# When the weight sums of an attention and feed-forward kernel may begin, and where in the third tile they stand

## The chip, the cores and the metric

One core of a Trainium2 chip runs the kernel. The metric is device time in microseconds (us). Engines: PE multiplies matrices, DVE (VectorE) and ACT (ScalarE) work element by element, POOL (GpSimd) and SP (SyncE) here mostly issue DMA transfers. Each engine takes its instructions strictly in the order of its own queue.

## The reference

```python
# attention in chunks of 64 positions, 8 x 8 heads, 576 positions, 64 wide
scores = scale * np.matmul(q_c, k_c.transpose(0, 1, 2, 4, 3))
scores = scores - np.max(scores, axis=-1, keepdims=True)
attn = np.exp(scores)
attn = attn / (np.sum(attn, axis=-1, keepdims=True) + 1e-09)
out = np.matmul(attn, v_c)
# its output becomes x, 4608 tokens x 512; w_in is 512 x 2048, w_out 2048 x 512
h = x @ w_in
g = np.where(h >= 1, h, np.where(h <= -1, 0.0, (h + 1) ** 2 / 4))
return (g @ w_out).astype(np.float32)
```

Everything is float32.

## The kernel before, in words

**Tiles.** The 4608 tokens are nine tiles of 512. For each the attention of its heads is computed, then h and g in 16 slices of 128 columns, j = 0 to 15, then the output. Each float32 factor is split into a high and a low part, and three products (high with high, high with low, low with high) replace one. `ffn_in` (line 610) issues the 12 products of a slice into a bank `ps_h`; ACT and DVE make g from it in a buffer `r` (lines 617, 620, 621); `ffn_split` makes its high part `gh` on ACT (line 629) and the low part `gl` on DVE (line 631); `ffn_out` (line 646) adds 12 products into four banks `ps_o`, two slices later. There are two buffers each of `ps_h`, `r`, `gh` and `gl`. I write I0, I1, ... and O0, O1, ... for input and output products, numbered 16 t + j: I16 and O16 are the first of tile 1, O32 the first of tile 2. V and S are the value and score products of the attention for coming tiles, put in between as bursts; each burst is followed by a row maximum (`mx`), eight exponentials on ACT, sums (`sm`) and transposes on DVE, and small moves of the results (`aT`, line 565, on POOL or SP).

**Two ways of multiplying.** Tiles 0, 1 and 2 are computed as said. Tiles 3 to 8 go in pairs by a scheme with seven products in place of eight, which needs sums and differences of blocks of the weights. These are made during tiles 1 and 2, each from two slices of a weight: `combine_weights(p)` for w_in, p = 0 to 7, called w0 to w7 below, and `combine_out(p)` for w_out, called o0 to o5 (two more follow in tile 3). Each consists of two first adds on DVE, four half-width adds, two roundings on ACT, two subtractions on DVE (lines 728 and 732), and then stores to DRAM that POOL issues: seven for w (line 838, four from the staging tiles and three of raw weight parts), four for o (line 986). Besides, `keep_factor` (line 961) stores 24 raw pieces of w_out to DRAM. Tile 3 and later load all of it back through rings.

**Staging tiles.** The sums are made in four tiles of 128 x 512, `tmp0` to `tmp3`, in two pairs (shown as `tmp_135` and `tmp_136`). The same four receive the output of tiles 0, 1 and 2 from `ps_o` (`store`, DVE line 660, ACT line 662), from where SP stores it (line 667); a bank `ps_o` is free for the next tile once its copy is made. Banks 0 and 3 are copied into pair 0, banks 1 and 2 into pair 1; banks 0 and 2 by ACT, 1 and 3 by DVE. In tile 2 every second sum uses another pair of stages, `alt` (`new_wi_0`, `new_wi_1`), instead: those whose step is in `AGAIN`.

**What sets the order.** All work is first recorded with `plan.add(engine, cost, emit, reads, writes, ...)`. `Plan.emit` then runs a simple simulation: an entry becomes ready when the entries that wrote its keys are done, and each engine takes, of its ready entries, the one with the smallest turn, which is its place in the record less `ahead`. Sums of w_out and raw stores have `ahead=LATER`, that is 60 places behind. The order in which the plan takes entries is the order of the hardware queues. On the chip an instruction waits for the data that it reads and the buffers that it writes. The step of the record is (t - 1) * 16 + j; the main loop calls the sums at the steps in `SUMS_AT` and `WEIGHTS`:

```python
ffn_split(t, j)
if step in WEIGHTS:
    combine_weights(WEIGHTS.index(step), step in AGAIN)
if step in SUMS_AT:
    combine_out(SUMS_AT.index(step), step in AGAIN)
if t == 1:
    for name in ("P4",) if j % 2 else ("P1", "P2"):
        keep_factor(name, j // 2)
```

In the record a raw store thus stands in tile 1, but it reads only a slice of w_out that was prepared in tile 0, so the plan may take it as soon as POOL has nothing else ready.

Of the kernel before, what the change touches and what calls it, by code (L numbers as in the profile page):

```python
# [9 lines left out]
F32 = mybir.dt.float32  # L10
# [123 lines left out]
def kernel(  # L134
# [15 lines left out]
    nc = tc.nc  # L150
# [85 lines left out]
    weight = {}  # L236
# [27 lines left out]
    plan = Plan()  # L264
# [3 lines left out]
    def now(ap):  # L268
        return ap() if callable(ap) else ap
# [355 lines left out]
    def ffn_split(t, j, source=None, ahead=0):  # L625
        rkey, r = source or r_bufs[j % 2]
        ghkey, gh = gh_bufs[j % 2]
        glkey, gl = gl_bufs[j % 2]
        plan.add("act", 0.52, lambda: nc.scalar.copy(out=gh, in_=now(r)), (rkey,), (ghkey,),  # L629
                 ahead=ahead)  # L630
        plan.add("dve", 0.6, lambda: nc.vector.tensor_tensor(  # L631
            out=gl, in0=now(r), in1=gh.bitcast(F32), op=ALU.subtract
        ), (rkey, ghkey), (glkey,), port=True, ahead=ahead)
# [85 lines left out]
    def cols(n):  # L719
        return slice(n * QC, (n + 1) * QC)  # L720
# [5 lines left out]
    def act_copy(cost, out, src, reads, writes, ahead=0):  # L726
        plan.add(
            "act", cost, lambda: nc.scalar.copy(out=out(), in_=src()), reads, writes, ahead=ahead  # L728
        )
# [59 lines left out]
    def stage_of(again):  # L789
        if again:  # L790
            some = [(f"alt{n}_{i}", part_of(f"alt{n}", i)) for n in range(2) for i in range(2)]
            return *some, [lambda n=n: held[f"alt{n}"] for n in range(2)]
        return *((key, fixed(ap)) for key, ap in tmp_bufs), [fixed(pair) for pair in tmp_pairs]

    def combine_weights(p, again=False):
        js = (2 * p, 2 * p + 1)
        keys = [[f"wi{j}_{n}" for n in range(2)] for j in js]
        (k1, w1), (k12, s12), (k2, w2), (k34, s34), pairs = stage_of(again)

        def kc(ap, n):  # L800
            return lambda: ap().rearrange("p (i two f) -> p two i f", i=2, two=2)[:, n]

        def two(ap, n):
            return lambda: ap()[:, cols(n)].rearrange("p (i f) -> p i f", i=2)

        for j, ks, key, w in zip(js, keys, (k1, k2), (w1, w2)):
            dve(0.6, ALU.add, w, lambda j=j: weight["wi", j][:, 0, :].bitcast(F32),
                lambda j=j: weight["wi", j][:, 1, :].bitcast(F32), ks, (key,))
        a11, a12, a21, a22 = (kc(w, n) for w in (w1, w2) for n in range(2))
        dve(0.34, ALU.add, two(s12, 0), a21, a22, (k2,), (k12,))  # L810
        dve(0.34, ALU.subtract, two(s12, 1), two(s12, 0), a11, (k1,), (k12,))
        dve(0.34, ALU.subtract, two(s34, 0), a11, a21, (k1, k2), (k34,))
        dve(0.34, ALU.subtract, two(s34, 1), a12, two(s12, 1), (k1, k12), (k34,))
        for hkey, hi, key, ap in ((k1, w1, k12, s12), (k2, w2, k34, s34)):
            act_copy(0.52, rounded(hi), ap, (key,), (hkey,))
            dve(0.6, ALU.subtract, rounded(ap), ap, hi, (hkey,), (key, f"split_{p}"))
        st = [(k1, k12), (k2, k34)]

        def of_block(n, h):
            return lambda: weight["wi", js[n]].rearrange(  # L820
                "p x (i two f) -> p two x i f", i=2, two=2
            )[:, h]

        def of_stage(n, h):
            return lambda: pairs[n]()[:, :, cols(h)].rearrange("p x (i f) -> p x i f", i=2)

        for r, src, reads in (
            (2, of_stage(0, 1), st[0]), (3, of_stage(0, 0), st[0]),
            (5, of_stage(1, 0), st[1]), (4, of_stage(1, 1), st[1]),
            (0, of_block(0, 0), (*keys[0], f"split_{p}")), (1, of_block(0, 1), (*keys[0], f"split_{p}")),  # L830
            (6, of_block(1, 1), (*keys[1], f"split_{p}")),
        ):
            d, n = divmod(7 * p + r, 2)

            def send(d=d, n=n, src=src):
                dst = combos[d][:, n, :].rearrange("p (x i f) -> p x i f", x=2, i=2)
                ap = src()
                nc.gpsimd.dma_start(out=dst.bitcast(F32), in_=ap.bitcast(F32))

            plan.add("pool", 0.7, send, reads, (f"dram{d}_{n}",), lag=1.7, moving=0.8)  # L840
# [112 lines left out]
        for name in OUT_ORDER for p in range(NQ)  # L953
    }

    def keep_factor(name, p):
        n, half = RAW[name]
        j = 2 * p + n

        def send():  # L960
            nc.gpsimd.dma_start(  # L961
                out=sums[name, p].bitcast(F32), in_=weight["wo", j][:, :, cols(half)].bitcast(F32)
            )

        plan.add("pool", 0.7, send, (f"wo{j}_0", f"wo{j}_1"), (f"sums_{name}_{p}",), lag=3.0,
                 moving=0.8, ahead=LATER)

    def combine_out(p, again=False, behind=()):
# [343 lines left out]

    SPREAD = {1: (None, 8), 4: (8, 9), 7: (9, 10), 10: (10, 11), 13: (11, 12), 15: (None, 13)}
    SPREAD.update({NF + 2 * n: (12 + n, 14 + n) for n in range(8)})
    SUMS_AT = (0, 6, 12, 18, 20, 23)
    WEIGHTS = (2, 4, 8, 10, 14, 21, 26, 28)
    AGAIN = sorted(step for step in (*SUMS_AT, *WEIGHTS) if step > 17)[::2]

    def burst(n, m):
# [15 lines left out]
    for t in range(ALONE + 1):  # L1335
        for j in range(NF):
            step = (t - 1) * NF + j
            if t == 0:
                for what, g in SECOND.get(j, ()):
                    what(*divmod(NP + g, NP))  # L1340
            elif step in SPREAD:
                n, m = SPREAD[step]
                if n is None and m == 2 * NP:
                    attn_turn(*AT[m])
                burst(n, m)
                if m is not None and m + 1 <= 3 * NP + 1:
                    attn_turn(*AT[m + 1])
            ffn_in(t, j)
            prepare_next()
            m = t * NF + j - LAG  # L1350
            if m >= 0:
                ffn_out(*divmod(m, NF))
            ffn_split(t, j)
            if step in WEIGHTS:
                combine_weights(WEIGHTS.index(step), step in AGAIN)
            if step in SUMS_AT:
                combine_out(SUMS_AT.index(step), step in AGAIN)
            if t == 1:
                for name in ("P4",) if j % 2 else ("P1", "P2"):
                    keep_factor(name, j // 2)  # L1360
            if t == ALONE and j < len(HANDED):
                hand_lot("wi", j, F32 if j < 2 else F32R, *HANDED[j])
                if j == 2:
                    hand_lot("wo", 0, F32R, "ring0")
        if t:
            take_raws((first_raw, next_raw)[t - 1], t % 2)
# [17 lines left out]
    for t in range(ALONE + 1, NTILE, 2):  # L1384
        if t > ALONE + 1:
            move_blocks()
        for n, (p, name) in enumerate(alternating(0, NQ)):
            between(n)
            if t == ALONE + 1 and name == "P1":
                if p in (1, 4):  # L1390
                    combine_out(len(SUMS_AT) + p // 4, True, (blocks["eA", p - 1][0],))
                place_blocks(p)
# [69 lines left out]
```

## Time and profile before

| what | us |
|---|---|
| three runs | 819.76, 821.46, 821.82; median 821.46 |
| the profiled execution | 822.29 |
| its span in the trace | 820.5 |
| busy: PE, DVE, ACT, POOL | 808.1, 659.1, 537.6, 343.6 |
| first input product of tile 1 / of tile 2 | 126.87 / 222.17 |
| last output product of tile 2 ends | 326.24 |

The stretches are read as shares: PE busy for the whole of a slice means that nothing is lost there. A bracket at the end of a timeline row, [1.62 <-DMA ...], is the idle time of that engine ahead of the row, and what ended it. A DMA row at POOL or SP is the issue; when the data has landed is told by the DMA table, as a median per kind.

### The profile page before, as it was taken

To read this page: it belongs to the slowest core of one execution; us is meant where nothing else is said; L and a number is where in the kernel's file an instruction comes from. 1 tells how busy PE (TensorE), PEld (TensorE's weight loads), DVE (VectorE), ACT (ScalarE), POOL (GpSimd) and SP (SyncE) were. 2 spreads that over 40 slices of the span, in tenths; PEclk is the share of its full clock that TensorE was granted. 3 is DMA by queue.
4 is the path that set the end of the run, shared out by engine and by line. 5 is a ranking of instruction groups with operands and counts; after the bars stand their busy time and mean duration, and the time that the engine had idled before them with its cause. 6 is when DMAs were issued, how large, how long until landed. Compare 5 with 4: busy or idle time off the path is not lost.

```text
span 820.5 us, 18541 instructions
## 1 busy us (share of the span) xinstructions
PE 808.1 (98%) x6464; PEld 694.1 (85%) x6464; DVE 659.1 (80%) x1143; ACT 537.6 (66%) x1295; POOL 343.6 (42%) x606
## 2 busy tenths in 40 slices
PE   8999999999999999999999999999999999999998
PEld 7777778888888788878899998878999988888887
DVE  4999998778889986888899885778995845589963
ACT  5789876455676765778985446778844456686450
POOL 2133343345446463556454333554433333333330
PEclk9999999999999999999999999999999999999999
DMA  9999955765798796999999678987666876666673
GB/s 216 265 309 289 301 134 156 204 196 173 195 259 236 197 278 150 282 272 283 272 240 271 184 236 241 249 229 220 191 200 186 228 219 197 194 192 186 208 208 109
DMA packets 245356, 181.61 MB, mean 221 GB/s; under 512 B 192656, under 2 KB 210576, under 8 KB 245264
## 3 DMA queue, kind: packets, MB, share of 16 engines
q0 software_dynamic: 40640, 122.72, 48.0%
q1 hardware_dynamic: 202512, 57.18, 30.7%
q8 instruction: 52, 0.85, 0.4%
q10 hardware_dynamic: 2112, 0.52, 0.3%
q14 instruction: 40, 0.33, 0.2%
HBM read 133.17 MB, written 38.80 MB: 210 GB/s over the span
## 4 chain that ended last, share of the span: by engine, by line
PE 75%; DMA 9%; DVE 5%; SPq 5%; issue 2%; ACT 1%; POOL 1%; DVEq 0%; POOLq 0%; ACTq 0%
PE ps_o L1119 19%; PE ps_h L610 12%; PE ps_o L646 11%; PE ps_o L903 10%; PE ps_h L903 10%; PE ps_h L1119 8%; DMA q_sb<-in_q_dram 3%; PE ps_a L1119 3%; DMA words<-in_moe_w_in_dram 2%; SPq L382 2%; PE ps_a L487 2%; DMA k_sb<-in_k_dram 1%; PE ps_a L465 1%; DMA v_sb<-in_v_dram 1%; SPq L398 1%
## 5 line engine op out<-in xcount | busy, mean ns | idle before, releaser
L728 ACT CAST new_wi<-new_wi 128x512 fp32r<-128x512 f32 x156 | 94.5, 625 | 63.6 <-PE ps_o L1119 32.2
L732 DVE TENSOR_TENSOR new_wi<-new_wi,new_wi 128x512 fp32r<-128x512 f32 (+2 forms) x194 | 124.8, 673 | 13.2 <-ACT new_wi L728 12.9
L610 PE MATMUL ps_h<-xh,parts 128*128 128x512 f32 x384 | 130.0, 398 | 3.2 <-DVE parts L350 1.7
L646 PE MATMUL ps_o<-parts,gh 128*128 128x512 f32 x384 | 118.6, 390 | 0.0
L610 PEld LDWEIGHTS ps_h<-xh,parts 128*128 128x128 f32 x384 | 71.9, 188 | 20.1 <-DVE parts L350 2.6
L646 PEld LDWEIGHTS ps_o<-parts,gh 128*128 128x128 f32 x384 | 72.0, 188 | 14.9
L646 PE MATMUL ps_o<-parts,gl 128*128 128x512 f32 x192 | 74.8, 390 | 0.3 <-DVE gl L631 0.3
L565 POOL DMA_DIRECT2D aT<-e x96 | 48.2, 511 | 46.3 <-issue 13.6
L934 DVE SCALAR_TENSOR_TENSOR new_wi<-h,new_wi 128x512 f32<-128x512 f32 x62 | 41.8, 685 | 30.4 <-ACT new_wi L933 30.3
L532 ACT ACTIVATE e<-ps_a,mx 128x64 f32<-128x64 f32 x168 | 50.6, 328 | 11.6 <-DVE mx L526 8.2
L933 ACT ACTIVATE new_wi<-new_wi 128x512 f32<-128x512 f32 x84 | 51.6, 638 | 1.0
L610 PE MATMUL ps_h<-x_parts,parts 128*128 128x512 f32 x128 | 50.1, 392 | 0.0
L930 ACT ACTIVATE new_wi<-h 128x512 f32<-128x512 f32 x62 | 38.9, 641 | 13.0 <-DVE h L924 12.8
L629 ACT CAST gh<-r 128x512 fp32r<-128x512 f32 x48 | 29.9, 624 | 26.6 <-DVE r L621 18.9
L646 PEld LDWEIGHTS ps_o<-parts,gl 128*128 128x128 f32 x192 | 36.1, 188 | 8.3 <-DVE gl L631 0.8
L961 POOL DMA_DIRECT2D sums_P<-parts x24 | 17.8, 789 | 57.5 <-DVE parts L350 57.5
L732 DVE TENSOR_TENSOR new_wi<-new_wi 128x512 f32<-128x512 f32 (+2 forms) x64 | 40.2, 631 | 0.4
L631 DVE TENSOR_TENSOR gl<-r,gh 128x512 fp32r<-128x512 f32 x48 | 32.7, 684 | 7.6 <-ACT gh L629 7.0
L621 DVE SCALAR_TENSOR_TENSOR r<-ps_h,r 128x512 f32<-128x512 f32 x48 | 32.7, 683 | 7.2 <-ACT r L620 7.0
L532 ACT ACTIVATION_READ_ACCUMULATOR e<-ps_a,mx 128x1 f32 x168 | 37.2, 221 | 0.0
L1119 PE MATMUL ps_o<-new_wo,new_wi 128*128 128x256 f32 (+1 forms) x244 | 35.0, 293 | 0.0
L1119 PE MATMUL ps_o<-ring_r,new_wi 128*128 128x256 f32 (+1 forms) x244 | 34.6, 293 | 0.0
(260 smaller groups left out, 2158.8 us busy)
## 6 DMA issues: line engine op xcount, KB each, us to landing
ring_r<-combos POOLq DMA_DIRECT2D x36, 256.0 KB, 3.8
new_wo<-sums_P POOLq DMA_DIRECT2D x36, 256.0 KB, 3.3
new_wi<-combos POOLq DMA_DIRECT2D x34, 256.0 KB, 4.6
new_wi<-sums_P POOLq DMA_DIRECT2D x34, 256.0 KB, 3.2
ring_gh<-combos POOLq DMA_DIRECT2D x33, 256.0 KB, 4.0
ring_gl<-combos POOLq DMA_DIRECT2D x33, 256.0 KB, 3.9
ring_gh<-sums_P POOLq DMA_DIRECT2D x33, 256.0 KB, 3.3
ring_gl<-sums_P POOLq DMA_DIRECT2D x33, 256.0 KB, 3.5
```

Source lines behind the costliest of these rows:

```text
L532: nc.scalar.activation(out=e3[:, n, :], in_=sc[:, n // 4, n % 4, :], func=AF.Exp, bias=mx[:, n, :], scale=SCALE, accum_out=sm[:, n, :],)
L565: queues[queue].dma_start(out=aT[b:b + Q, to], in_=x[a:a + Q, of])
L610: nc.tensor.matmul(out=ps, lhsT=weight["wi", j][:, half, kc * P:(kc + 1) * P], rhs=x, start=(kc == 0 and i == 0), stop=(kc == KC - 1 and i ...
L621: plan.add("dve", 0.6, lambda: nc.vector.scalar_tensor_tensor(out=r, in0=ps, scalar=1.0, in1=r, op0=ALU.max, op1=ALU.min), (pkey,), (rkey,))
L646: nc.tensor.matmul(out=acc, lhsT=x[:, cols], rhs=weight["wo", j][:, half, :], start=(j == 0 and i == 0), stop=(j == NF - 1 and i == 2),)
L728: "act", cost, lambda: nc.scalar.copy(out=out(), in_=src()), reads, writes, ahead=ahead
L732: plan.add("dve", cost, lambda: nc.vector.tensor_tensor(out=out(), in0=one(), in1=two(), op=op), reads, writes, port=True, ahead=ahead)
L903: nc.tensor.matmul(out=ps, lhsT=w()[:, at:at + P], rhs=y(), start=name in FRESH and i == 0 and k == 0, stop=i == 1 and k == 2, skip_group_ ...
L930: plan.add("act", 0.52, lambda: nc.scalar.activation(out=now(r), in_=h(), func=AF.Relu, bias=0.5, scale=0.5), (hkey,), (rkey,), ahead=50)
L933: plan.add("act", 0.52, lambda: nc.scalar.square(out=now(r), in_=now(r)), (), (rkey,), ahead=50)
L934: plan.add("dve", 0.6, lambda: nc.vector.scalar_tensor_tensor(out=now(r), in0=h(), scalar=1.0, in1=now(r), op0=ALU.max, op1=ALU.min), (hke ...
L1119: nc.tensor.matmul(out=into, lhsT=x()[:, block], rhs=factor, start=first and k == 0, stop=p == NQ - 1 and k == len(steps) - 1, skip_group_ ...
```

## The change

`ffn_split`'s ACT copy now also writes a key `split_t_j`. The first adds of `combine_weights` and of `combine_out`, and the raw stores of `keep_factor`, read the key of the step at which they are recorded. In the plan, and by the wait that follows from it on the chip, they can't begin before the `gh` copy of that step. Two tables change: the sums o4 and o5 go from steps 20 and 23 to 23 and 28, w5, w6 and w7 from 21, 26 and 28 to 20, 25 and 30. In tile 2, steps 16 to 31, the sums then stand at 18, 20, 23, 25, 28 and 30. `AGAIN` follows from the tables: before {18, 21, 26} used the `alt` stages, after it is {18, 23, 28}. No instruction is added or removed.

```diff
@@ ffn_split
-        plan.add("act", 0.52, lambda: nc.scalar.copy(out=gh, in_=now(r)), (rkey,), (ghkey,),
-                 ahead=ahead)
+        plan.add("act", 0.52, lambda: nc.scalar.copy(out=gh, in_=now(r)), (rkey,),
+                 (ghkey, f"split_{t}_{j}"), ahead=ahead)
@@ combine_weights
-    def combine_weights(p, again=False):
+    def combine_weights(p, again=False, behind=()):
...
-                lambda j=j: weight["wi", j][:, 1, :].bitcast(F32), ks, (key,))
+                lambda j=j: weight["wi", j][:, 1, :].bitcast(F32), (*ks, *behind), (key,))
@@ keep_factor
-    def keep_factor(name, p):
+    def keep_factor(name, p, behind):
...
-        plan.add("pool", 0.7, send, (f"wo{j}_0", f"wo{j}_1"), (f"sums_{name}_{p}",), lag=3.0,
+        plan.add("pool", 0.7, send, (f"wo{j}_0", f"wo{j}_1", behind), (f"sums_{name}_{p}",), lag=3.0,
                  moving=0.8, ahead=LATER)
@@ the main loop
-    SUMS_AT = (0, 6, 12, 18, 20, 23)
-    WEIGHTS = (2, 4, 8, 10, 14, 21, 26, 28)
+    SUMS_AT = (0, 6, 12, 18, 23, 28)
+    WEIGHTS = (2, 4, 8, 10, 14, 20, 25, 30)
...
-                combine_weights(WEIGHTS.index(step), step in AGAIN)
+                combine_weights(WEIGHTS.index(step), step in AGAIN, (f"split_{t}_{j}",))
             if step in SUMS_AT:
-                combine_out(SUMS_AT.index(step), step in AGAIN)
+                combine_out(SUMS_AT.index(step), step in AGAIN, (f"split_{t}_{j}",))
             if t == 1:
                 for name in ("P4",) if j % 2 else ("P1", "P2"):
-                    keep_factor(name, j // 2)
+                    keep_factor(name, j // 2, f"split_{t}_{j}")
```

What this moves in the queues is shown at three places, each before and after. First POOL in tile 0: L961 are the raw stores of w_out (`sums_P_p` is their place in DRAM, `parts` a prepared weight), L565 the moves `aT` of the attention, L986 the stores of o0. Before:

```order
L961 DMA sums_P_0_148<-parts_463 256x1x256
L556 TENSOR_TENSOR first_144<-first_144,sm_84 128x512
L961 DMA sums_P_0_156<-parts_655 256x1x256
L961 DMA sums_P_0_180<-parts_655 256x1x256
L961 DMA sums_P_1_149<-parts_722 256x1x256
L565 DMA aT_78<-e_76 32x256 x8
L961 DMA sums_P_1_157<-parts_811 256x1x256
L961 DMA sums_P_1_181<-parts_811 256x1x256
L565 DMA aT_79<-x_80 32x256 x8
```

After:

```order
L556 TENSOR_TENSOR first_144<-first_144,sm_84 128x512
L565 DMA aT_78<-e_76 32x256 x8
L565 DMA aT_79<-x_80 32x256 x8
L565 DMA aT_78<-e_77 32x256 x8
L565 DMA aT_79<-e_76 32x256 x8
L961 DMA sums_P_0_148<-parts_463 256x1x256
L961 DMA sums_P_0_156<-parts_654 256x1x256
L986 DMA sums_P_0_188<-tmp_135 256x1x256
L565 DMA aT_78<-x_80 32x256 x4
```

All four groups of eight `aT` moves now stand ahead of the first raw store, and o0's stores and the raw stores of tile 1's first steps come together behind them.

Then PE at the passage from tile 1 to tile 2, behind the burst V and S: the end of I34 (`ps_h_141`), and O32 (`gh_131`, `gl_133`, into `ps_o_139`, `140` and the double bank `137`). Before:

```order
L610 MATMUL ps_h_141<-xh_0_93,parts_564 128x512
L610 MATMUL ps_h_141<-x_parts_86,parts_564 128x512
L610 MATMUL ps_h_141<-xh_0_93,parts_564 128x512
L646 MATMUL ps_o_139<-parts_463,gh_131 128x512 x2
L646 MATMUL ps_o_139<-parts_463,gl_133 128x512
L646 MATMUL ps_o_140<-parts_463,gh_131 128x512 x2
L646 MATMUL ps_o_140<-parts_463,gl_133 128x512
```

After:

```order
L610 MATMUL ps_h_141<-xh_0_93,parts_563 128x512
L610 MATMUL ps_h_141<-x_parts_86,parts_563 128x512
L610 MATMUL ps_h_141<-xh_0_93,parts_563 128x512
L610 MATMUL ps_h_142<-xh_0_87,parts_654 128x512
L610 MATMUL ps_h_142<-x_parts_85,parts_654 128x512
L610 MATMUL ps_h_142<-xh_0_87,parts_654 128x512
L646 MATMUL ps_o_139<-parts_463,gh_131 128x512 x2
L646 MATMUL ps_o_139<-parts_463,gl_133 128x512
L646 MATMUL ps_o_137<-parts_463,gh_131 128x512 x2
L646 MATMUL ps_o_137<-parts_463,gl_133 128x512
L610 MATMUL ps_h_142<-xh_0_89,parts_654 128x512
L610 MATMUL ps_h_142<-x_parts_85,parts_654 128x512
```

Three products of I35 (`ps_h_142`) now stand ahead of O32, and three more in its middle, ahead of its products into the bank `ps_o_140`; the passage from tile 0 to 1 is alike, with I19, I20, V, S and three products of I21 ahead of O16, which before stood between I18 and I19.

Last DVE at the same place, around the two copies L660 of tile 1's output out of `ps_o`. Before:

```order
L631 TENSOR_TENSOR gl_133<-r_129,gh_131 128x512
L556 TENSOR_TENSOR e_77<-e_77,sm_83 128x512
L621 SCALAR_TENSOR_TENSOR r_130<-ps_h_142,r_130 128x512
L573 STREAM_TRANSPOSE x_80<-e_77 128x8x2x32
L660 COPY tmp_136<-ps_o_140 128x512
L660 COPY tmp_135<-ps_o_137 128x512
L631 TENSOR_TENSOR gl_134<-r_130,gh_132 128x512
L732 TENSOR_TENSOR new_wi_1_2616<-parts_1081 128x512
L521 TENSOR_REDUCE mx_82<-ps_a 128x8
```

After:

```order
L732 TENSOR_TENSOR tmp_136<-tmp_136 128x512
L621 SCALAR_TENSOR_TENSOR r_130<-ps_h_142,r_130 128x512
L732 TENSOR_TENSOR xl_1_96<-raw_2420,xl_1_95 128x512
L631 TENSOR_TENSOR gl_134<-r_130,gh_132 128x512
L521 TENSOR_REDUCE mx_82<-ps_a 128x8
L441 STREAM_TRANSPOSE qT_74<-q_sb_68 128x512
L660 COPY tmp_135<-ps_o_137 128x512
L526 TENSOR_SCALAR mx_82<-mx_82 128x8
L441 STREAM_TRANSPOSE kT_75<-k_sb_70 128x512
L732 TENSOR_TENSOR raw_2420<-raw_2421,raw_2420 128x512
L660 COPY tmp_136<-ps_o_140 128x512
```

The last subtraction of w4 (`tmp_136<-tmp_136`), which before stood far ahead, now comes shortly before the copies, and a row maximum, two transposes and a subtraction of the next burst stand ahead of the second copy.

## Rows read from the trace of the kernel before

**Rows 1.** The whole core by stretches: start:end, length, then busy time per engine

```profile
core 0: us, PE busy (x) PEld busy (x) DVE busy (x) ACT busy (x) POOL busy (x), PEclk, DMA share, GB/s
...
82.00:102.50 20.50, 19.28 (x141) 14.99 (x140) 20.43 (x30) 18.19 (x37) 7.96 (x13) 1.00 1.03 300
...
123.00:143.50 20.50, 20.50 (x120) 16.76 (x119) 17.53 (x31) 12.64 (x33) 6.95 (x11) 1.00 0.57 157
...
225.50:246.00 20.50, 20.50 (x181) 16.66 (x182) 18.43 (x38) 14.76 (x51) 9.86 (x17) 1.00 0.95 259
...
266.50:287.00 20.50, 19.71 (x205) 15.97 (x204) 20.06 (x42) 14.80 (x45) 9.39 (x18) 1.00 0.77 196
...
328.00:820.50 492.50, 487.98 (x3779) 432.36 (x3778) 381.34 (x656) 313.98 (x723) 208.24 (x389) 1.00 0.79 221
```

**Rows 2.** Waits of PE, 123 to 330 us

```profile
PE ps_h L610 <- DVE r L621: 0.8, 1, 0.8
```

**Rows 3.** Timeline of PE: start us, us, engine, line, operation [idle before]

```profile
141.32 0.39 PE L646 MATMUL ps_o<-parts,gh 128*128 128x512 f32 x1
...
149.58 0.69 PE L487 MATMUL ps_a<-aT,v_sb 64*64 64x64 f32 x32
...
237.22 0.62 PE L646 MATMUL ps_o<-parts,gh 128*128 128x512 f32 x2
...
271.83 0.50 PE L610 MATMUL ps_h<-xh,parts 128*128 128x512 f32 x1 [0.79 <-DVE r L621]
...
327.60 2.88 PE L903 MATMUL ps_h<-new_wi,new_wi 128*128 128x512 f32 x12
330.32 0.84 PE L903 MATMUL ps_o<-xl,ring_r 128*128 128x512 f32 x3
```

**Rows 4.** DMA issues by kind: queue, count, KB each, median us to landing

```profile
sums_P<-parts POOLq DMA_DIRECT2D x24, 256.0 KB, 5.2
combos<-tmp POOLq DMA_DIRECT2D x24, 256.0 KB, 4.2
...
sums_P<-tmp POOLq DMA_DIRECT2D x20, 256.0 KB, 3.7
```

**Rows 5.** Timeline of ACT

```profile
35.85 1.15 ACT L323 ACTIVATE tmp<-words 128x1024 f32<-128x1024 f32 x1 [1.62 <-DMA words<-in_moe_w_in_dram]
...
231.89 0.59 ACT L662 COPY tmp<-ps_o 128x512 f32<-128x512 f32 x1
...
234.94 0.59 ACT L662 COPY tmp<-ps_o 128x512 f32<-128x512 f32 x1 [2.46 <-DMA combos<-tmp]
```

**Rows 6.** Timeline of DVE

```profile
37.03 0.70 DVE L326 TENSOR_SCALAR tmp<-tmp 128x1024 uint32<-128x1024 uint32 x1 [0.38 <-ACT tmp L323]
...
38.27 1.23 DVE L333 CUSTOM_DVE_ANT_0 tmp<-words,tmp 128x2048 uint16<-128x2048 uint16 x1 [0.54 <-ACT words L329]
...
128.03 0.65 DVE L732 TENSOR_TENSOR tmp<-parts 128x512 f32<-128x512 f32 x1
...
150.72 0.69 DVE L732 TENSOR_TENSOR tmp<-parts 128x512 f32<-128x512 f32 x1
...
162.12 0.69 DVE L732 TENSOR_TENSOR tmp<-parts 128x512 f32<-128x512 f32 x1 [0.57 <-DMA combos<-tmp]
...
219.57 0.69 DVE L732 TENSOR_TENSOR tmp<-parts 128x512 f32<-128x512 f32 x1 [1.17 <-DMA sums_P<-tmp]
...
234.96 1.29 DVE L660 COPY tmp<-ps_o 128x512 f32<-128x512 f32 x2 [1.31 <-DMA combos<-tmp]
```

**Rows 7.** Timeline of POOL, the issues of stores

```profile
132.97 2.83 POOL L986 DMA_DIRECT2D sums_P<-tmp  x4 [4.27 <-DVE tmp L732]
...
155.29 2.92 POOL L838 DMA_DIRECT2D combos<-tmp  x4 [12.41 <-DVE tmp L732]
...
227.36 2.91 POOL L838 DMA_DIRECT2D combos<-tmp  x4 [1.44 <-DVE mx L526]
...
297.73 2.89 POOL L838 DMA_DIRECT2D combos<-tmp  x4 [0.42 <-DVE tmp L732]
```

## The prediction

> **What bounds the kernel now.** I read the table by stretches first. From 123 us on the reader sees TensorE (PE) busy for 20.50 us of every 20.50, but for one slice, 266.5 to 287.0, with 19.71; after 328 it is busy 487.98 of 492.5; in tile 0, before 123, VectorE (DVE) sets the pace instead: 20.43 of 20.50 in the slice that begins at 82.0, where PE has 19.28 [rows 1]. [...] The waits of PE between 123 and 330 are a single one, 0.8 us before an input product, on DVE's `r` [rows 2]; in the timeline it is the row at 271.83 with 0.79 us idle [rows 3]. So tiles 1 and 2 and the passage into tile 3, where everything that the diff touches now lies, are a PE stream with 0.79 us to give back. What can be lost is larger: every wait put into that stream counts in full.
>
> **The change, part by part.** No instruction is added or taken away; the gates move DVE sums, ACT roundings and POOL stores later, and the tables move o4, o5 and w5 to w7 within tile 2. I call the sums of the output weights o0 to o5 and those of the input weights w0 to w7.
>
> Tile 0. 24 raw stores of 256 KB [rows 4], 6.3 MB, leave it: POOL now sends the four groups of `aT` first, and the raw stores come in tile 1. What they hid behind or held up there is small. Until DVE saturates, one word tile makes ACT wait, 1.62 us on its DMA at 35.85 [rows 5], and DVE's idle time after it is 0.38 and 0.54 us [rows 6]. If the lighter DMA load removes that, 0.9 us comes back; if later DVE work takes it, nothing. I take 0.4. Afterwards DVE has the same work in the same order, so its 20.43 of 20.50 stays.
>
> Passage of tile 0 to 1. DVE began o0 at 128.03 [rows 6]; now it waits for the gh copy of step 0, about 132.4, and shares DVE with an attention burst, so o0's four stores go at about 139.7 to 143.8 instead of from 132.97 [rows 7]. Their staging tiles are those into which tile 0's output is copied, so the copies come when the stores have landed: 143.8 plus the median of 3.7 [rows 4] is 147.5, and with the DVE copies behind a row maximum 148.9 to 149.5. Output products O16 stood at 141.32 [rows 3]. PE now does 27 input products first, 27 x 2.72/12 (the row of 12 products at 327.60 to the next at 330.32 [rows 3]) = 6.1 us, and an attention burst of two groups of at most 0.69 each: it comes to O16 at about 148.6. Stall 0 to 1.0; I take 0.2, because the late bank is the second one needed.
>
> Tile 1, the chain through the staging tiles. Two pairs of tiles serve every sum, so each sum waits until the stores of the one before have landed: in five of the eight sums of tile 1 DVE waits for such a landing, first 0.57 us at 162.12 and last 1.17 at 219.57 [rows 6]. A late start is therefore not made up. I walked it with the durations of these rows: the output copies go out at about 150 rather than 143, w0's second add moves from 150.72 [rows 6] to about 159.0 behind the r and gl of step 4, its stores from 155.29 [rows 7] to 162.3. From there the cycles of my walk, of 13.0, 9.9, 12.9, 11.6, 11.2 and 11.9 us, put w4's stores at 232.8, against 227.36 [rows 7]: 5.4 us late, as 1.6 of the 7.0 is won back where DVE had waited. One group of `aT` goes behind w1's stores and costs PE 0 to 0.3; I take 0.2.
>
> Passage of tile 1 to 2. Here the chain meets PE. Before, ACT waited 2.46 us for w4's stores at 234.94 [rows 5], DVE 1.31 us and copied until 236.25 [rows 6], and O32 began at 237.22 [rows 3]: a margin of 1.0 us. In that place the last store needed from 229.55 (three store pitches behind 227.36) to 234.9, 5.3 us; the median of such stores is 4.2 [rows 4]. With stores 5.4 us later and 5.3 us of landing, pair 0 (second store at 233.5) is free at 238.8, the ACT copy ends at 239.5, and PE, which the new order brings to O32 three products later, at 237.9, waits 1.7 us. Then it has nine products (2.0 us) ahead of the first bank of pair 1; that pair lands at 240.3, its DVE copy, now behind a maximum, a transpose and a subtraction, ends at about 241.8: 0.2 more. Sum 1.9. With a landing of 3.8 it would be 0.4, and with the chain 3 us later still, 5; with the chain only 3 us late, none. I take 1.9, since w4's own landing is the nearest row, and keep 0 to 5.
>
> The row shows 5.3 and 4.2 us for 256 KB. [...]
>
> Tile 2. o4, o5 and w5 to w7 stand at steps 20, 23, 25, 28, 30 instead of 20, 21, 23, 26, 28, and DVE is less crowded where it was busy 20.06 of 20.50 [rows 1]. The r that was late at 271.83 comes, by my walk, at about 271 and is needed at 273.4. Gain 0.8; it stays zero if another sum takes its place.
>
> Passage of tile 2 to 3. w7's stores, at 297.73 before [rows 7], now wait for the split of step 30, about 318.5, and in POOL's queue behind a ring load: about 324 to 329, landed by 329 to 332. Tile 2's last output copies need those staging tiles, and tile 3's first product into the first bank is at 330.32 [rows 3], into the second 4 us later. Cost 0 to 1; I take 0.4. The ring loads queued behind w7's stores start some 5 us later and still land ahead of their products.
>
> Sum: -0.4 +0.2 +0.2 +1.9 -0.8 +0.4 = +1.5 us on the profiled execution of 822.29 (span 820.5 and 1.8 around it), 823.8. That execution lay 0.83 above the median 821.46, so the median becomes 823.0. A measurement of this kernel can tell 0.3%, 2.46 us: faster is below 819.0, slower above 823.92.
>
> **The rivals.**
> A, slower: the stores that left tile 0 lengthen the landings in tile 1. 24 x 256 KB now share that tile, whose last stretch already had a DMA share of 0.95 [rows 1]. The eight landings of the chain at 0.4 us more each make w4 another 3 us later, the wait at O32 becomes 5, and the sum +4.6, or 826 for the median; with a little more at the passage to tile 3, 826.5. It decides from the point where w4's last store is issued later than about 236. For it speaks that the raw stores have the longest landing, 5.2 us [rows 4]; against it that the share of DMA in the first slice of tile 1 was 0.57 [rows 1].
> B, nothing lost: the chain makes up its delay in tile 1, since DVE is no longer saturated (17.53 of 20.50 [rows 1]), and O32 sees its copies in time. Then -0.4 -0.8 = -1.2: 820.3. Against it stand the landing waits [rows 6].
> C, faster: tile 0 is bound by its transfers more than by DVE, and the 6.3 MB give PE back what it lacks there. The DMA share is 1.03 where PE is 19.28 [rows 1], so that slice lacks 1.22 us; if three slices like it get that back, 3.7, and the 0.8 of tile 2 comes too, less 0.8 for the smaller terms and 0.4 for a short landing at O32, the sum is -3.3 and the median 818.2. Against it: DVE is full there and its order does not change.
> That the gates do not bind is part of B: from w1 on the chain is later than its steps anyway, so only o0, the raw stores and tile 2 move; this changes no number above, as o0's delay alone starts the walk.
>
> **How the numbers follow.** The forecast gets 0.50, A 0.22, B 0.18, C 0.10. The forecast's own range is 821.5 to 825. The range for 8 in 10 takes in B and A, 819.6 to 827.0, and leaves C out. Faster: C and a little of B, 0.12. Within 0.3%: 0.36 of the forecast and 0.16 of B, 0.52. Slower: A and 0.14 of the forecast, 0.36.
>
> **What would show it.** The profile after must have a PE wait of 1 to 3 us before an output product (ps_o, first of tile 2) on the copies into ps_o's staging, near 238; a first group of o0's stores near 139.7 and w4's near 232.8; no wait near 271.8; landings of the L838 stores of 4 to 5.5 us. If PE's busy time in the slices before 123 rises by more than 1 us, C is right; if the stores of w4 go before 230 and no wait stands at 238, B; if they go after 236, A. A wait of PE between 148 and 152 above 1 us, or one in tile 2 that was not there, would make the step in question wrong.

## The result, and the profile after

The changed kernel is slower: 829.77 us median of 6 runs (828.08 to 832.28), the kernel before beside it 821.32 (6 runs), ratio 1.0107, 95% interval 1.0086 to 1.0128. The forecast was 823.0, 1.5 us slower, with a range up to 827.0; the sign was right, but the size was 8.45 us. The profiled execution took 830.29, its span 828.5, which is 8.0 more than before.

The waits of PE in the profile after, from 130 to 400 us (engine, what it waited for, us in total, times, longest):

```profile
PE ps_a L487 <- ACT x L532: 3.7, 1, 3.7
PE ps_a L487 <- DMA q_sb<-in_q_dram: 2.0, 1, 2.0
PE ps_h L903 <- ACT new_wi L930: 1.2, 1, 1.2
PE ps_h L610 <- DVE r L621: 0.6, 1, 0.6
PE ps_o L646 <- DVE tmp L660: 0.2, 1, 0.2
```

Before there was one wait up to the entry of tile 3 [rows 2]. Now the place that I forecast, output products (ps_o, L646) behind their copies, has 0.2 us. The large wait is an attention product V (L487) that may not overwrite its bank `ps_a` before ACT's exponentials (L532) have read it. The timeline of PE has the rows (start, us, operation, [idle before]):

```profile
215.02 0.50 PE L610 MATMUL ps_h<-xh,parts 128*128 128x512 f32 x1 [0.60 <-DVE r L621]
...
222.43 0.39 PE L610 MATMUL ps_h<-xh,parts 128*128 128x512 f32 x1
226.54 1.23 PE L487 MATMUL ps_a<-aT,v_sb 64*64 64x64 f32 x29 [3.72 <-ACT x L532]
...
246.32 0.73 PE L646 MATMUL ps_o<-parts,gh 128*128 128x512 f32 x2 [0.20 <-DVE tmp L660]
...
342.71 1.61 PE L903 MATMUL ps_h<-new_wi,ring_gh 128*128 128x512 f32 x6 [1.18 <-ACT new_wi L930]
...
365.33 0.86 PE L487 MATMUL ps_a<-aT,v_sb 64*64 64x64 f32 x29 [2.01 <-DMA q_sb<-in_q_dram]
```

**What the wait costs beyond itself.** The same stretch in short slices (start:end, length, busy PE, PEld, DVE, ACT, POOL, granted clock, DMA share, GB/s):

```profile
215.00:220.00 5.00, 4.98 (x22) 4.12 (x23) 2.93 (x5) 2.38 (x4) 4.20 (x8) 1.00 1.04 338
222.00:224.00 2.00, 0.81 (x4) 0.35 (x2) 2.00 (x6) 1.03 (x5) 1.08 (x2) 1.00 0.75 302
224.00:226.00 2.00, 0.00 (x0) 0.00 (x0) 1.81 (x3) 2.00 (x13) 0.58 (x2) 0.81 0.74 181
226.00:228.00 2.00, 1.46 (x50) 1.47 (x53) 1.36 (x5) 1.00 (x5) 2.00 (x4) 0.50 0.82 212
228.00:230.00 2.00, 2.00 (x29) 1.69 (x24) 1.88 (x4) 0.62 (x1) 0.61 (x2) 0.50 1.06 313
230.00:232.00 2.00, 2.00 (x6) 1.52 (x6) 2.00 (x5) 1.66 (x4) 2.00 (x5) 0.50 1.00 283
232.00:234.00 2.00, 2.00 (x11) 1.65 (x10) 2.00 (x5) 2.00 (x13) 0.36 (x1) 0.98 0.74 220
```

PE stood still from 222.82 to 226.54; the granted clock was 0.81 in the slice 224 to 226, 0.50 in the three from 226 to 232 and 0.98 in the next; the slices of before have 1.00 [rows 1]. From 226.54 to 232.0 PE was busy, but its products of 128 x 512 began 0.43 us apart (229.25 and 229.68), and 0.23 apart behind it (233.53 and 233.76):

```profile
229.25 0.63 PE L610 MATMUL ps_h<-x_parts,parts 128*128 128x512 f32 x1
229.68 0.63 PE L610 MATMUL ps_h<-xh,parts 128*128 128x512 f32 x1
...
233.53 0.39 PE L646 MATMUL ps_o<-parts,gl 128*128 128x512 f32 x1
233.76 0.39 PE L610 MATMUL ps_h<-xh,parts 128*128 128x512 f32 x1
```

So it did about half of its work: by an estimate, busy time times what the clock lacked of 1.00, 5.46 x 0.5 = 2.7 us were lost on top of the 3.72. A row that says "busy 2.00 of 2.00" hides this; of the columns above only the clock's shows it.

**Who held V.** DVE and ACT ahead of it:

```profile
218.94 0.69 DVE L732 TENSOR_TENSOR tmp<-parts 128x512 f32<-128x512 f32 x1 [2.00 <-DMA combos<-tmp]
219.55 0.69 DVE L631 TENSOR_TENSOR gl<-r,gh 128x512 fp32r<-128x512 f32 x1
220.64 0.69 DVE L732 TENSOR_TENSOR tmp<-parts 128x512 f32<-128x512 f32 x1 [0.40 <-DMA combos<-tmp]
221.25 0.42 DVE L732 TENSOR_TENSOR tmp<-tmp 128x256 f32<-128x256 f32 x1
221.58 0.42 DVE L732 TENSOR_TENSOR tmp<-tmp,tmp 128x256 f32<-128x256 f32 x1
221.92 0.68 DVE L521 TENSOR_REDUCE mx<-ps_a 128x8 f32<-128x512 f32 x1
```

```profile
222.97 0.62 ACT L728 CAST tmp<-tmp 128x512 fp32r<-128x512 f32 x1 [4.22 <-DVE tmp L732]
223.49 0.31 ACT L532 ACTIVATE x<-ps_a,mx 128x64 f32<-128x64 f32 x1
```

The first two adds of o2 (218.94, 220.64) wait for the stores of w3; the row maximum `mx` of the burst stands behind them in DVE's queue, though its scores were done at 214.4; ACT's exponentials stand behind o2's rounding; V stands behind the exponentials. DVE was late here because the chain was late. The groups of stores on POOL, which answer to [rows 7]:

```profile
139.25 0.69 POOL L986 DMA_DIRECT2D sums_P<-tmp  x1 [28.82 <-DVE tmp L732]
...
162.29 2.90 POOL L838 DMA_DIRECT2D combos<-tmp  x4 [3.58 <-DVE tmp L732]
...
185.07 2.84 POOL L986 DMA_DIRECT2D sums_P<-tmp  x4 [0.64 <-DVE tmp L732]
...
212.50 2.89 POOL L838 DMA_DIRECT2D combos<-tmp  x4 [5.36 <-DVE tmp L732]
...
225.42 2.83 POOL L986 DMA_DIRECT2D sums_P<-tmp  x4 [2.35 <-DVE tmp L732]
...
238.80 2.90 POOL L838 DMA_DIRECT2D combos<-tmp  x4 [6.44 <-DVE tmp L732]
...
330.58 2.91 POOL L838 DMA_DIRECT2D combos<-tmp  x4 [0.64 <-DVE tmp L732]
```

**The entry of tile 3.** w7's stores, at 297.73 before [rows 7], are the row 330.58. SP's queue before and after (issue start, time of the group):

```profile
325.02 5.07 SPq L671 DMA_DIRECT2D out_dram<-tmp  x8
...
343.11 3.65 SPq L565 DMA_DIRECT2D aT<-e  x4
```

```profile
335.02 7.63 SPq L671 DMA_DIRECT2D out_dram<-tmp  x8
...
356.84 3.28 SPq L565 DMA_DIRECT2D aT<-e  x4
```

The first pair is before, the second after. The output stores of tile 2 come 10.0 us later and the `aT` moves queued behind them 13.7 later, while PE's last output product is only 5.7 later (331.67 against 326.02). V at 365.33 waits 2.01 us; the profile names the load of q as the last to come, the `aT` moves stand in the same queue. (L671 is the line of tile 2's output stores.) The 1.18 us at 342.71 ended with ACT's copy L930; what made that copy late is not shown.

The account of the 8.0 us: -1.1 in tile 0 (its first product of tile 1 with `xl` starts at 125.96, before 127.10), +0.6 (215.02), +3.72, +2.7 by the clock (the estimate), +0.2, -0.79 (the wait at 271.83 is gone), +1.18, +2.01, -0.6 for two waits that before had in tile 3. That is 7.9.

### The profile page after: what moved, and what is told of

Same layout as the page of the kernel before. It is cut to its first block, busy times and chain, and to the rows that moved or that the text cites. A ratio compares the mean times of both kernels' runs of the same rounds, so it can differ in the third digit from the quotient of the medians.

```text
span 828.5 us, 18531 instructions
## 1 busy us (share of the span) xinstructions
PE 812.1 (98%) x6464; PEld 698.6 (84%) x6464; DVE 660.1 (80%) x1143; ACT 537.7 (65%) x1295; POOL 343.0 (41%) x606
## 4 chain that ended last, share of the span: by engine, by line
PE 57%; DVE 2%; DMA 2%; ACT 1%; issue 1%; POOL 0%; SPq 0%; DVEq 0%; ACTq 0%; POOLq 0%
PE ps_o L1119 19%; PE ps_o L903 13%; PE ps_h L903 13%; PE ps_h L1119 8%; PE ps_a L1119 3%; PE ps_a L487 1%; DVE new_wi L732 1%; PE ps_a L465 1%; DMA aT<-e 1%; ACT e L532 1%; DMA q_sb<-in_q_dram 0%; DVE tmp L732 0%; DMA combos<-tmp 0%; DMA ring_r<-combos 0%; POOL combos L838 0%
## 5 line engine op out<-in xcount | busy, mean ns | idle before, releaser
L732 DVE TENSOR_TENSOR new_wi<-new_wi,new_wi 128x512 fp32r<-128x512 f32 (+2 forms) x196 | 125.5, 669 | 13.3 <-ACT new_wi L728 12.9
L646 PE MATMUL ps_o<-parts,gh 128*128 128x512 f32 x384 | 119.4, 392 | 0.2 <-DVE tmp L660 0.2
L646 PEld LDWEIGHTS ps_o<-parts,gh 128*128 128x128 f32 x384 | 72.4, 189 | 15.9 <-DVE tmp L660 0.6
L565 POOL DMA_DIRECT2D aT<-e x96 | 48.4, 510 | 81.4 <-ACT tmp L323 34.3
L646 PE MATMUL ps_o<-parts,gl 128*128 128x512 f32 x192 | 74.9, 390 | 0.0
L532 ACT ACTIVATE e<-ps_a,mx 128x64 f32<-128x64 f32 x168 | 50.8, 331 | 11.8 <-DVE mx L526 8.2
L930 ACT ACTIVATE new_wi<-h 128x512 f32<-128x512 f32 x62 | 38.8, 640 | 15.9 <-DVE h L924 15.6
L617 ACT ACTIVATE r<-ps_h 128x512 f32<-128x512 f32 x48 | 29.1, 606 | 21.3 <-PE ps_h L610 21.0
L646 PEld LDWEIGHTS ps_o<-parts,gl 128*128 128x128 f32 x192 | 36.3, 189 | 7.6
L532 ACT ACTIVATION_READ_ACCUMULATOR e<-ps_a,mx 128x1 f32 x168 | 37.5, 223 | 0.0
L838 POOL DMA_DIRECT2D combos<-tmp x32 | 23.3, 730 | 31.0 <-DVE tmp L732 25.8
L565 POOL DMA_DIRECT2D aT<-x x48 | 24.3, 517 | 26.1 <-issue 9.7
```

What stands on the lines that cost most here:

```text
L532: nc.scalar.activation(out=e3[:, n, :], in_=sc[:, n // 4, n % 4, :], func=AF.Exp, bias=mx[:, n, :], scale=SCALE, accum_out=sm[:, n, :],)
L565: queues[queue].dma_start(out=aT[b:b + Q, to], in_=x[a:a + Q, of])
L646: nc.tensor.matmul(out=acc, lhsT=x[:, cols], rhs=weight["wo", j][:, half, :], start=(j == 0 and i == 0), stop=(j == NF - 1 and i == 2),)
L732: plan.add("dve", cost, lambda: nc.vector.tensor_tensor(out=out(), in0=one(), in1=two(), op=op), reads, writes, port=True, ahead=ahead)
L930: plan.add("act", 0.52, lambda: nc.scalar.activation(out=now(r), in_=h(), func=AF.Relu, bias=0.5, scale=0.5), (hkey,), (rkey,), ahead=50)
```

## The experiments

Each kernel ran beside the kernel before, and the ratio is to that: four executions each, six of the changed kernel, ten of e1, e3 and e13. Two figures from each profile place the loss: from the first `xl` product of tile 1 to the start of the last output product of tile 2, and from there to the end of the span.

| kernel | median us | ratio, 95% interval | tiles 1 and 2 | to the end |
|---|---|---|---|---|
| before | 821.3 | 1 | 198.9 | 494.5 |
| changed | 829.8 | 1.0107, 1.0086 to 1.0128 | 205.7 | 496.8 |
| e1 tables alone | 822.0 | 1.0006, 0.9994 to 1.0017 | 198.3 | 494.5 |
| e2 raw stores free | 830.6 | 1.0100, 1.0076 to 1.0124 | 202.4 | 499.4 |
| e3 raw stores gated alone | 822.0 | 1.0011, 0.9998 to 1.0025 | 200.4 | 494.3 |
| e4 o0 free | 828.0 | 1.0078, 1.0063 to 1.0093 | 200.7 | 498.7 |
| e5 maximum ahead of o2 | 828.8 | 1.0086, 1.0054 to 1.0117 | 203.4 | 496.6 |
| e7 gates in tile 1 only | 827.5 | 1.0074, 1.0050 to 1.0099 | 205.5 | 494.1 |
| e8 gates in tile 2 only | 827.1 | 1.0064, 1.0039 to 1.0089 | 198.2 | 500.9 |
| e9 w7 on the alt stages | 831.0 | 1.0115, 1.0087 to 1.0144 | 205.3 | 498.7 |
| e10 w7 free | 830.0 | 1.0102, 1.0087 to 1.0117 | 209.0 | 494.1 |
| e11 all gates, old tables | 832.5 | 1.0129, 1.0112 to 1.0147 | 210.5 | 494.2 |
| e12 e5 and e7 together | 829.1 | 1.0093, 1.0078 to 1.0108 | 208.0 | 494.2 |
| e13 o0's gate alone | 824.7 | 1.0040, 1.0026 to 1.0054 | 201.2 | 494.4 |

A single profile places a loss; the ratio, from all runs, sizes it. The start of tile 1 itself lay between 124.1 and 128.0 us in the nine profiles without raw stores in tile 0 (median 126.0) and between 125.5 and 128.3 in the five with them (median 127.6). The two ranges overlap, so the -1.1 above is not shown to be the change's.

**Which part of the change costs: e1 to e4.** e1 is before with the two new tables. e2 is the changed kernel with

```diff
-        plan.add("pool", 0.7, send, (f"wo{j}_0", f"wo{j}_1", behind), ...
+        plan.add("pool", 0.7, send, (f"wo{j}_0", f"wo{j}_1"), ...
```

e3 is before with that gate alone, and e4 the changed kernel with

```diff
-    combine_out(..., step in AGAIN, (f"split_{t}_{j}",))
+    combine_out(..., step in AGAIN, (f"split_{t}_{j}",) if step else ())
```

> Only the two step tables are changed (o4, o5, w5 to w7 at their new steps), no gates. Theory 1 (the long wait of 3.7 us before V at the first burst of tile 2, and the half clock behind it, come from the gates in tile 1): no such wait, clock 1.00, and only what the tables do in tile 2 and at the entry of tile 3 is left: the 0.8 us wait gone, up to 3.2 us added at the entry, 820.5 to 824. Theory 2 (the tables are the cause): 827 to 830.

> The changed kernel, but the 24 raw stores are not gated, so they go back to tile 0. Theory 1a (the sums' late start makes the chain late): the V wait of about 3 us or more and a slice at half clock stay, 827 to 831. Theory 1b (6.3 MB of raw stores in tile 1 lengthen the landings and with them the chain): the V wait goes, clock 1.00, 822 to 825 with only the entry of tile 3 left over.

> The kernel before, and only the raw stores gated (old tables, sums free). Theory 1a: no V wait; the 1.1 us that tile 0 gained stays, 820 to 821.5. Theory 1b: landings in tile 1 grow to 5 us and more, w3's and o2's adds wait 2 us each, a V wait of 2 us or more with a half clock behind it, 825 to 829.

> The changed kernel with a single gate left out, that of o0 (step 0). Theory 1a in its narrow form (the chain is late because of o0's late start alone): o0's stores near 133, w3's near 205 rather than 212.5, no V wait, 822 to 825. If the later gates or the raw stores keep the chain late, w3's stores stay after 210 and the time at 828 to 831.

The tables and the raw stores alone are each within the measurement of before; the gates of the sums cost, with the raw stores in either tile. e3 fits neither branch: V waits 0.99 us, where 1a had no wait and 1b 2 us and more, and its profile begins tile 1 2.0 us earlier and loses 1.5 of them in tiles 1 and 2. e2 contradicts both theories as I wrote them: the time stays, but not by the V wait. There the loss in tiles 1 and 2 sits at O32, where I had forecast it, and the clock falls behind it:

```profile
240.38 0.72 PE L646 MATMUL ps_o<-parts,gh 128*128 128x512 f32 x2 [0.56 <-ACT tmp L662]
...
242.33 0.73 PE L646 MATMUL ps_o<-parts,gh 128*128 128x512 f32 x2 [0.99 <-ACT tmp L662]
```

```profile
242.00:244.00 2.00, 1.67 (x5) 1.33 (x6) 1.35 (x4) 1.97 (x11) 0.22 (x1) 0.77 0.90 244
244.00:246.00 2.00, 2.00 (x6) 1.58 (x5) 1.89 (x3) 1.07 (x2) 0.00 (x0) 0.50 1.09 350
246.00:248.00 2.00, 2.00 (x9) 1.59 (x9) 1.82 (x4) 0.17 (x1) 1.76 (x4) 0.88 1.06 326
```

Two waits of 1.55 us together, then slices at 0.77, 0.50 and 0.88: by the same estimate about 0.4 + 1.0 + 0.2 = 1.6 more. The rest of e2 is at the entry of tile 3, a V wait of 4.10 us at 365.57. e4 fell between its two branches: w3's stores at 205.49, as the narrow form had it, and only 1.04 us before V, but its time stayed at 828.01 by the entry of tile 3 (waits of 1.46 and 2.09, the clock at 0.50 behind the second). So there are two costs, and each is taken by itself below.

**Does the order on DVE and ACT make the V wait: e5.** The changed kernel; while the plan gives out its order, o2's pieces are kept back until the burst's exponentials and transposes have been given out:

```diff
...
+            if self.tags[n] == "late" and not released:
+                kept_back.append(emit)
+            else:
+                emit()
...
```

> The changed kernel with one edit of the queues: on DVE the two first adds and the first two half adds of o2 stand behind the row maximum, its scaling and the transposes of the burst at the end of tile 1, and on ACT o2's two roundings behind that burst's exponentials; every other order is the changed kernel's. Theory 1 (V at the first burst of tile 2 waits because this maximum stands behind o2's adds, which wait for w3's stores): the 3.7 us wait falls below 1.5, the clock stays at 1.00 there, and the time falls by 4 to 6.5 us, to 824 to 826. If aT's landing or w3 itself holds V, the wait and the time stay, 828 to 831.

The mechanism holds, the gain does not follow. V's wait fell to 0.56 us, and the loss came back at O32, which PE now reached in time to wait (in this kernel line 500 is V, 661 the output product, 675 and 677 its copies):

```profile
221.19 0.86 PE L500 MATMUL ps_a<-aT,v_sb 64*64 64x64 f32 x29 [0.56 <-DVE tmp L747]
...
239.07 0.73 PE L661 MATMUL ps_o<-parts,gh 128*128 128x512 f32 x2 [2.08 <-ACT tmp L677]
...
242.10 0.72 PE L661 MATMUL ps_o<-parts,gh 128*128 128x512 f32 x2 [0.69 <-DVE tmp L675]
```

The median, 828.79, missed the 824 to 826. The four executions spread from 825.93, the profiled one with a clock of 1.000, to 831.54; the other three had 0.997 and 0.998. A fall of the clock is thus not there in every execution, and it is part of the spread; where it fell in the three that were not profiled is not recorded.

**The entry of tile 3: e7 to e11.** e7 drops the gates for t = 2, e8 keeps only those, with the raw stores free as well; e9 swaps the stages, e10 frees w7, e11 is the changed kernel with the old tables:

```diff
e7: step in AGAIN, (f"split_{t}_{j}",) if t == 1 else ()
e9: AGAIN = sorted(...)[1::2]
e10: combine_weights(..., (f"split_{t}_{j}",) if step < 30 else ())
```

> The changed kernel with the gates of tile 2 left out (sums of steps 16 to 30 free), those of tile 1 and the raw stores kept. If the entry of tile 3 is late because w7's gate puts its stores into the staging tiles that tile 2's output needs: SP's output stores come within 1 us of PE's own shift after 325, no PE waits between 335 and 370, and the wait at the first burst of tile 2 stays: 825.5 to 828. If the entry is late for another reason, 829 to 831.

> The new tables, and gates only for the sums of tile 2; raw stores and the sums of tile 1 free. By the theory of two separate costs only the entry of tile 3 is paid: tile 2's output stores on SP near 333 to 335 instead of 325, PE waits of 2 us or more between 338 and 366, 823.5 to 826.5. If the gates of tile 2 cost nothing by themselves, 820.5 to 822.5.

> The changed kernel with the other half of tile 2's sums on the alt stages (steps 20, 25, 30 instead of 18, 23, 28), so that w7 uses no tile that tile 2's output is copied into. If the entry of tile 3 is late through those tiles: SP's output stores follow the last output product within 4 us (about 329 to 331), no waits at 342 and 365, 826 to 828, the wait at the first burst of tile 2 unchanged. If it is late through the transfers themselves (w7's seven stores and the loads at one time), the waits stay and 829 to 831.

> The changed kernel with the gate of w7 alone (step 30) left out; it then goes ahead of o5. If w7's late stores alone make the entry of tile 3 late: no PE wait above 0.5 us between 335 and 370, SP's output stores within 5 us of the last output product, 826 to 828.5, the wait of 3 us or more at the first burst of tile 2 still there. If o5's gate or the others do it too, waits of 1 to 3 us remain and 828.5 to 831.

> All gates, but the old tables (o4, o5 at 20 and 23, w5 to w7 at 21, 26, 28). The gates of tile 1 are the same, so the wait at the first burst of tile 2 and the slice at half clock stay (827 or more); w7 may begin two steps (11 us) earlier, so its stores leave before the entry of tile 3: no waits there, 826 to 828.5. If the time is 829 to 831, the entry doesn't depend on w7's step.

e7 and e8 cut the cost in two: without gates in tile 2 the rest of the run takes 494.1 us, as before, and V's wait of 3.46 us stays; with these gates alone tiles 1 and 2 take 198.2, as before, and one V waits 4.58 us at the entry, with the clock at 0.50 behind it:

```profile
362.40 0.86 PE L487 MATMUL ps_a<-aT,v_sb 64*64 64x64 f32 x29 [4.58 <-DMA aT<-e]
```

e8's time, 827.09, lies 0.6 us above its branch, and its output stores began at 329.42, earlier than the 333 to 335 expected. e9 goes against the staging tiles as the whole reason. With w7 on other stages SP's output stores did start early, at 330.25, before the last output product, and the wait near 365 was gone; but their eight issues took 10.27 us, PE waited for a ring load, and the time did not fall:

```profile
330.25 10.27 SPq L671 DMA_DIRECT2D out_dram<-tmp  x8
```

```profile
344.46 2.90 PE L903 MATMUL ps_h<-new_wi,ring_gh 128*128 128x512 f32 x6 [3.34 <-DMA ring_gh<-combos]
```

What the runs with a costly entry share (changed, e2, e4, e8, e9; e5 the same) is w7's seven stores, which begin 1.1 to 1.4 us before tile 2's last output product; in the runs without it (e7, e10, e11) they are all issued 10 us and more before that product. In e2, e4, e5 and e8 the profile names `aT` itself as what V waits for there. Whether w7's stores delay the ring loads in POOL's queue, or the transfers on both queues, is left open. e10 and e11 took that cost away and were no faster, so both missed their times, 829.96 and 832.45 in place of 826 to 828.5: V still waits 3.07 and 3.51 us, and besides e10 waits 1.81 us at 326.75 and e11 2.79 us at 280.06, each with slices at 0.50 behind it. In these two kernels the gates of tile 2 that are left cost as much at another place.

**Both costs taken away, and o0's gate by itself: e12, e13.**

> The changed kernel with both costs taken away: o2's four adds and two roundings behind the burst at the end of tile 1, and no gates in tile 2. The two-cost account gives no wait above 1 us at V near 221, none between 335 and 370, and what is left is the wait at O32 of 1 to 3 us (with or without a fall of the clock behind it): 822 to 825.5. If something else makes up the loss, 826 or more.

> The kernel before with one gate, that of o0 at step 0; old tables, raw stores and every other sum free. If o0's late start is enough to make the chain of staging tiles late through all of tile 1: o0's stores at 139 to 142, w4's at 232 or later, PE waits of 1 to 4 us in all at V near 222 or at O32 near 238 to 242, with or without a fall of the clock behind them, 823 to 826. If the chain makes up the delay when the raw stores stay in tile 0: w4's stores before 231, no wait there, 820.5 to 822.5.

e12 missed: the entry is free and V waits 1.08 us, but O32 now waits 2.21 and 1.71 us, and the clock falls behind it:

```profile
240.61 0.73 PE L661 MATMUL ps_o<-parts,gh 128*128 128x512 f32 x2 [2.21 <-ACT tmp L677]
...
243.28 1.22 PE L661 MATMUL ps_o<-parts,gh 128*128 128x512 f32 x2 [1.71 <-ACT tmp L677]
```

```profile
240.00:245.00 5.00, 2.68 (x7) 1.91 (x8) 4.01 (x10) 4.05 (x17) 3.04 (x6) 0.74 1.04 338
245.00:250.00 5.00, 5.00 (x14) 3.88 (x14) 3.62 (x8) 2.27 (x8) 1.75 (x4) 0.58 1.07 264
```

The slice from 245 has clock 0.58, by the same estimate 2.1 us lost. So in tiles 1 and 2 the cost is that the chain is late: in e5 and e12, where order took it away from V, PE met it at O32. e13 shows where it begins: one gate, on o0's two first adds at the start of tile 1, makes w4's stores leave at 231.76 rather than 227.36 [rows 7] and O32 wait

```profile
239.32 0.73 PE L646 MATMUL ps_o<-parts,gh 128*128 128x512 f32 x2 [1.41 <-ACT tmp L662]
```

with the clock at 1.000, for 0.40% (0.26 to 0.54). That is 3.3 us; the profiled execution, 822.89, was the fastest of the ten, so 1.41 us need not be the whole of it. With the raw stores in tile 1 as well (e7, the same tile 1 as the changed kernel) it is 0.74%. No version tried is faster than before.

**Two causes that meet in POOL's queue.** The profiles do not begin tile 1 at the same time, so the chain's lateness is taken from that start: us from the first `xl` product of tile 1 to the first store of a sum.

| kernel | o0 | o1 | w2 | w3 | w4 |
|---|---|---|---|---|---|
| before | 5.9 | 53.1 | 63.8 | 74.6 | 100.3 |
| e3 raw stores gated alone | 5.9 | 52.2 | 64.4 | 76.4 | 102.0 |
| e13 o0's gate alone | 13.3 | 59.0 | 70.5 | 81.0 | 106.2 |
| e2 all sums gated, raw stores free | 13.3 | 59.2 | 70.3 | 80.8 | 106.8 |
| changed | 13.3 | 59.1 | 73.9 | 86.5 | 112.8 |

o0's gate alone makes w4 6.0 us late, the raw stores alone 1.7, both together 12.6, more than their sum. The later gates add little in tile 1 (e2 beside e13). e2 and the changed kernel, which differ by the raw stores' gate alone, part at w2. POOL's rows of the changed kernel, and then of e2:

```profile
197.84 2.00 POOL L565 DMA_DIRECT2D aT<-x  x4 [7.79 <-issue]
199.83 2.93 POOL L838 DMA_DIRECT2D combos<-tmp  x4
```

```profile
198.55 2.87 POOL L838 DMA_DIRECT2D combos<-tmp  x4 [8.19 <-DVE tmp L732]
...
203.64 2.01 POOL L565 DMA_DIRECT2D aT<-x  x4
```

In the changed kernel w2's first subtraction on DVE ended at 196.47,

```profile
195.79 0.68 DVE L732 TENSOR_TENSOR tmp<-tmp 128x512 fp32r<-128x512 f32 x1
```

but four `aT` moves stand ahead of its stores in POOL's queue, and the stores left 3.4 us after it; in e2 POOL stood idle for 8.19 us until DVE released them, and the moves stand behind them. All seven kernels with o0's gate and the raw stores in tile 1 have this order, and none of the others has it. So more than half of the 6.0 us between e2 and the changed kernel is the order of a queue (3.6 at w2, 73.9 against 70.3). The rest comes at w3, whose stores follow w2's after 12.6 us, in e2 after 10.5; behind it o2's adds began 5.7 and 6.0 us behind the issue of the stores that they wait for. Longer landings are not general: the median of `combos<-tmp` between 150 and 245 us is 4.3 us before and 3.5 in the changed kernel.

## Why the prediction was wrong, step by step

The forecast was +1.5 us, the profile's account gives +7.9. Of the 6.4 between them 4.7 lie at the passage to tile 2 (1.9 forecast; 3.72 + 0.2 measured, 2.7 by the estimate) and 2.2 at the entry of tile 3 (0.4 forecast; 1.18 + 2.01 - 0.6 measured); the other terms make -0.5.

- **Tile 0 and the passage to tile 1.** O16 has no wait, and o0's stores began at 139.25, forecast 139.7; the walk of the chain held for w0 (162.29, forecast 162.3) and o1 (185.07, my walk 185.2). In part that is luck: tile 1 began 1.1 us earlier than in the profile that I walked from, so against its start these stores are about 1 us later than the walk. The sign that I gave for rival C, more than 1 us of PE's busy time before 123, came (115.9 before, 118.2 after), but it tells nothing of the raw stores: e13, with them in tile 0, began tile 1 at 125.53, and e4, without them, at 127.97.
- **The chain in tile 1: the first step that failed.** The walk is right for what it followed, o0's late start: against the start of tile 1 it had w4's stores at 105.7 (232.8 less 127.10), and in e13, with that gate alone, they left at 106.2. It failed where it took the 24 raw stores that now share the tile at nothing. Behind o1 it is short by 1.7, 2.8, 4.5 and 6.0 us for w2 (199.83), w3, o2 and w4: 238.80 instead of 232.8. Its cycle of 12.9 us from o1 to w2 took 14.8, since the new order has four `aT` moves ahead of w2's stores; o2's adds came at 218.94, 5.7 us behind the second store of w3 (212.50 and a pitch of 0.72), at a DMA share of 1.04. Rival A named the raw stores, and its sign came (w4's stores after 236), but its mechanism, eight landings longer by 0.4 us each, made 3 us; the raw stores brought 6.0 (changed beside e2), more than half of it by the order in POOL's queue.
- **What stands behind a waiting instruction: the second step that failed.** I followed o2's adds to O32 and not to the maximum behind them in DVE's queue. I named a row maximum ahead of an output copy, but not the adds ahead of a maximum. So the 1.9 us at O32 became 3.72 at V, and 0.2 at O32 because PE was late itself. With o0's gate alone the step was right in place and nearly in size: 1.41 at O32.
- **The clock: missing from the sum.** The rows of before have 1.00 everywhere [rows 1], and I took a wait at its own length and a slice full of PE's work as one without loss. After, the rows have 1.00 ahead of the wait of 3.72 us at V and 0.50 behind it, and by the estimate 2.7 us more went; behind 1.55 at O32 in e2 1.6 more. Rival A's wait of 5 us at O32 lacked this term as well.
- **The entry of tile 3: mis-sized.** w7's stores at 330.58 lie where I put them (324 to 329, with PE 5.7 us late), but the term of 0.4 was 1.18 + 2.01. I priced the output copies and the ring loads, and not SP's queue, where the `aT` moves came 13.7 us later, 8 more than PE's own delay; the 1.18 us, which ended with ACT's L930, I had not priced either.
- **Tile 2.** The 0.79 us at 271.83 went, as forecast. e1 shows that the tables alone bring nothing that can be measured.
- **The landing of a store.** I forecast 4 to 5.5 us for the stores L838. The median of `combos<-tmp` after is 3.5, and 5.7 to 6.0 went by where the chain was held, from w3's stores to o2's adds.

## What to carry to other kernels

Where a program fixes an in-order queue, a later start is followed through everything that stands behind the waiting instruction on its engine, not only through its own results: the dear consumer was here another chain (row maximum, exponentials, bank, V: 3.72 us, against 0.2 at O32). The stream that keeps TensorE full paid here a second price for a wait (2.7 us, by the estimate, behind 3.72): look up the clock behind every wait (the shortest here with a fall behind it was 1.55 us, in two pieces), and put what it costs into the sum. Two delays that are harmless or small alone can cross: the raw stores in tile 1 made w4 1.7 us late, but 6.0 once o0's gate had moved the sums behind other work in POOL's queue. When a fix removes a wait and the time stays, look for the next place at which the same late chain is met before calling the mechanism wrong.

## What the runs showed of the hardware that was not expected

In the slices the granted clock fell behind each of seven waits of PE of 2.8 us (e11, ending at 280.06) to 4.58 (e8) from tile 1 on: to 0.50 behind 2.8, 3.07 (e10), 3.72 (changed), 4.10 (e2) and 4.58, and to a mean of 0.66 and 0.54 over 5 us behind 3.46 (e7) and 3.51 (e11). Of e9, with waits of 3.58 and 3.34, no slices are given; its mean clock over the whole execution is 0.993. Around 2 us it went either way: it fell to 0.50 behind 1.81 (e10), 2.09 (e4) and 1.55 in two pieces (e2), and stayed at 1.00 in the profiled executions of e5 behind 2.08 and 0.69, and of the changed kernel behind 2.01 at 365. With 1.41 in e13 the mean of that execution was 1.000. What decides there is not shown.

What a fall cost did not follow the length of the wait. By the estimate above, over slices of 2 us or of 5 (e7, e12, and behind V in e10 and e11), it was 1.6 us behind 4.58 (e8) and 3.46 (e7), 2.7 behind 3.72 (changed) and 3.0 behind 3.07 (e10); the eleven falls that slices show lie between 1.6 and 3.0.

SP's eight issues of output stores took 5.0 to 5.1 us in the profiles of eight kernels without w7's stores beside them, and 6.29 (e2) to 10.27 (e9) in the six with them; by what way the one stretches the other is not shown.
